# Gated linear attention with a maxout layer: constants made on chip, wider rows for the output matrix, fewer memsets and a new order of the work

## The chip, the cores and the metric

The kernel runs on one core of one Trainium2 chip. The core has five engines that follow their own instruction queues: TensorE (PE in the profile, its weight loads PEld), VectorE (DVE), ScalarE (ACT), GpSimd (POOL) and SyncE (SP), which here issues every DMA. The metric is the device time of one execution in microseconds, lower is better. The kernel before took 142.0 us, the median of three runs (141.97, 142.00 and 146.79).

## The reference

Inputs are `q`, `k`, `v` and `alpha` of shape (4, 8, 768, 48): batch, heads, tokens, head width; all float32. Then come three matrices of 384 x 768 and one of 768 x 384.

```
state = zeros(B, H, D, D)
for t in range(S):
    state = alpha[:, :, t, :, None] * state + einsum('bhd,bhe->bhde', k[:, :, t], v[:, :, t])
    y[:, :, t] = einsum('bhd,bhde->bhe', q[:, :, t], state)
x = y.transpose(0, 2, 1, 3).reshape(3072, 384)
h = maximum(maximum(x @ w1, x @ w2), x @ w3)
out = h @ w_out
```

The recurrence is a gated linear attention: a 48 x 48 state per batch and head, decayed row by row with `alpha` at each token. The second part is a maxout layer over 3072 tokens.

## The kernel before

**Staging.** The tokens are cut into 12 steps: step `s` is batch `s % 4` and 256 tokens of it. Within a step the 128 partitions hold pairs of neighbouring tokens (R = 2), and a step has two chunks (U = 2) of 128 tokens, each 64 partitions. The kernel takes logarithms of alpha, sums them within a chunk by one matmul with a signed triangle (`upto`), and turns the sums into scales for k and q by Exp (`decay_in`, `decay_out`). Scaled q and k are transposed (`turn` on PE for steps 0 to 4, `turn_by_dma` for the rest), multiplied to scores, masked with a causal mask while they leave PSUM (`masked`), and multiplied with v (`attend`). Between chunks runs the state: `update`, `add_state`, `decay_state`, `spread_state`.

**The maxout layer.** `max(x w1, x w2, x w3)` is written as `x w1 + max(0, x (w2 - w1), x (w3 - w1))`. So the kernel forms two differences `wdif` (pieces d0 to d5, two for each group of 256 hidden columns), multiplies x with them (`gate`, pieces G0 to G5 per step, twelve matmuls each), takes the maximum with zero and with each other (`maxed`), and projects (`project`): the hidden part with `wo16`, and x itself with `w1o`, the product of w1 and w_out, formed once on chip (`turn_weight`, `multiply_weights`). A step's gates thus need the differences, and each difference two blocks of weights of 384 KB (pieces K0 to K8, K9 to K11 for w_out). The weight blocks are staged in the ring slots 2 and 3 that later hold inputs, so a load of step 2 or 3 into such a slot waits until the differences have read it.

**Order.** Nothing is scheduled automatically. The string `ORDER` lists some 900 pieces: a letter for the function, an index, an engine (`v` DVE, `p` POOL, `a` ACT), `@` the step, and `#` the PSUM banks. Each engine, SP included, executes its pieces in this order; semaphores are put in by the framework. `l0` to `l3` load alpha, k, q and v of a step; rings have four slots per input, so a load waits for the last reader of the step four before. `H` are warm-up matmuls on a tile of zeros without effect on the output.

**Constants.** `ca` (the triangle `upto`, the selector `pick` and three columns of scales) and `cb` (identity and causal mask `pmask`) are computed on the host as part of the program and loaded by the pieces J0 and J1, the second and fourth issues on SP. `rowmask`, the mask in the row order of step 0, is copied from `pmask` by ACT.

**Padding.** Heads take 48 of 64 columns; the rest is cleared once by `clear_padding`: sixteen memsets for the state tiles and two for `la` on DVE, eleven for `vu`, `qk` and `vt` on POOL. They stand ahead of everything else in these engines' queues.

Of the kernel before, what the change touches and what calls it, by code (L numbers as in the profile page):

```python
# [9 lines left out]
FP32 = mybir.dt.float32  # L10
FP16 = mybir.dt.float16

# [11 lines left out]
def kernel(  # L24
# [39 lines left out]
    rr = np.arange(P)  # L64
    tri_np = (
        ((rr[:, None] > MID) & (rr[:, None] <= rr[None, :])).astype(np.float16)
        - ((rr[:, None] <= MID) & (rr[:, None] > rr[None, :])).astype(np.float16)
    )
    w2_np = np.stack([rr <= MID, rr > MID], 1).astype(np.float16)
    ur, jr = rr // J, rr % J  # L70
    same = (ur[:, None] == ur[None, :]).astype(np.float16)
    upto_np = same * np.tile(tri_np[R - 1::R, R - 1::R], (U, U))
    pick_np = np.zeros((P, U, 2), np.float16)
    for u in range(U):
        pick_np[u * J:(u + 1) * J, u] = w2_np[::R]
    token = np.concatenate([R * np.arange(J) + r for r in range(R)])
    pmask_np = (token[:, None] <= token[None, :]).astype(np.float16)
    at_pair = LAM * (R * jr + R - 1 - MID)
    at_token = LAM * (rr // R * R + R - 1 - MID)
    c32_np = np.stack(  # L80
        [np.exp(at_pair + SIGMA), np.exp(-at_token - SIGMA), 0 * rr - LAM * P / 2], 1
    ).astype(np.float32)
    ca_np = np.concatenate([np.concatenate([upto_np, pick_np.reshape(P, -1)], 1).view(np.float32), c32_np], 1)
    cb_np = np.concatenate([np.eye(P, dtype=np.float16), pmask_np], 1)

# [40 lines left out]
    rowmask = cpool.tile([P, R, P], FP16, name="rowmask")  # L126

    def load_const(_, i, eng):
        c, c_np = ((ca, ca_np), (cb, cb_np))[i]
        queues[eng].dma_start(c, nc.inline_tensor(c_np, name=f"c{i}").ap())  # L130

    half = ca.bitcast(FP16)
    upto, pick = half[:, :P], half[:, P:P + 2 * U]
    c32 = ca[:, P // 2 + U:]
    ident, pmask = cb[:, :P], cb[:, P:2 * P]
    vs_c, ys_c, undo_c = c32[:, 0:1], c32[:, 1:2], c32[:, 2:3]
# [6 lines left out]
    sts = [[cpool.tile([P, HP, 2, D], FP16, name=f"st{b}_{i}") for i in range(2)] for b in range(B)]  # L143

    def clear_padding():
        for st in (st for pair in sts for st in pair):
            for i in range(2):
                nc.vector.memset(st[64 * i:64 * (i + 1), :, 1 - i], 0.0)
        for la in las:
            nc.vector.memset(la.rearrange("p r a b c -> p (r a b) c")[:, :, D:], 0.0)  # L150
        for vu in vus:
            nc.gpsimd.memset(vu.rearrange("p u a b c -> p (u a b) c")[:, :, D:], 0.0)
        for qk, vt in zip(qks, vts):
            nc.gpsimd.memset(qk.rearrange("p r i a b c -> p (r i a b) c")[:, :, D:], 0.0)
            nc.gpsimd.memset(vt.rearrange("p a b c -> p (a b) c")[:, :, D:], 0.0)


# [69 lines left out]
    def sums(s, *_):  # L227
# [4 lines left out]
        for p in range(HP):  # L232
            for n, (r, _) in enumerate(parts):
                nc.tensor.matmul(lps(s, 1)[:, H * D + 2 * U * p:H * D + 2 * U * (p + 1)],
                                 las[s % 2][:, r, p].rearrange("p a b -> p (a b)"), pick,
# [71 lines left out]
    def spread_mask(_, i, eng):  # L307
        for u in range(U):
            for r in range(R):
                copy(eng, rowmask[u * J:(u + 1) * J, r], pmask[r * J:(r + 1) * J])  # L310

    def masked(s, x, eng):
# [5 lines left out]
        else:  # L318
            nc.vector.tensor_mul(lats[s % 2][u][:, i], bank(("aps", s, u, i), [HP, P]),  # L319
                                 pmask.unsqueeze(1).broadcast_to([P, HP, P]))  # L320
# [95 lines left out]
    def differ(_, i, eng):  # L416
        jg, g = divmod(i, 2)
        engines[eng].tensor_sub(  # L418
            wdif[:, :, g, column_group(jg)], staged(3 * jg + 1 + g).rearrange("p (f j) -> p f j", f=NF),
            staged(3 * jg).rearrange("p (f j) -> p f j", f=NF))  # L420

    def halve(_, i, eng):
        copy(eng, w1h[i], staged(3 * i).rearrange("p (f j) -> p f j", f=NF))
# [98 lines left out]
    def warm_after(n, name):  # L522
# [5 lines left out]
        "l": load_step, "J": lambda _, i, eng: load_const(0, 1 - i, eng), "I": spread_mask, "K": load_weight, "H": warm,  # L528
# [9 lines left out]
    def emit(order):  # L538
# [24 lines left out]
        x1a@2 c0@3#7 M1v@0 C2v@0 n2a@0 G4@2#6 G1@2#3 u0v@4 C0a@0 m0p@5 h5v@0 G3@2#0 l2@3 s1v@2 G2@2#2 C1v@0
        f0a@3 h4a@1 z1v@0 P0@0#1 h2v@2 h3v@2 P1@0#5 l3@4 k0p@4 N0a@5 h5v@1 r0a@3 P2@0#2 h4v@2 p0a@0 l3@3 r1a@3
        p1a@0 c0@5#0 p2v@0 G0@2#4 e0a@5 O1@0#6 h0a@2 g0a@5 w0v@4 q0v@4 e0a@3 T1@4#1 g0a@3 u0v@3 O0@1#5 o1a@0
        k0v@3 l0@7 y1a@0 l1@5 w0v@3 f0a@5 l0@8 r0a@5 q0v@3 T0@4#2 o0a@1 G5@2#4 t1a@4 M1v@1 V0v@4 l0@6 T0@3#7
        V0v@3 O0@0#6 t0a@3 h1v@2 v0p@3 l3@5 t0v@4 h5v@2 S0@4#0,5 v0p@4 o0a@0 S0@3#1,7 s0v@4 A0@4#3,2 s0v@3 l3@6
        T1@3#4 M0v@3 a1v@4 z0p@4 O0@2#6 l1@6 t1a@3 a0v@4 s1v@4 z0p@3 y0a@3 s1v@3 W1@0 m0p@7 A1@4#0,1 y0a@4
        A1@3#2,4 a2v@3 A0@3#3,5 a1v@3 O1@2#7 a3v@4 r0a@7 m0p@6 N0a@7 a3v@3 V0a@5 l2@5 u0p@5 c0@7#2 l2@6 O1@1#5
        N0a@6 r1a@5 a2v@4 v1p@3 l0@9 a0v@3 v1a@4 Y0@4#1 o1v@1 k0p@5 m0p@8 Y3@3#4 Y0@3#0 Y2@3 o0v@2 x0a@3 Y1@4  # L570
        W0@0 Y3@4#3 Y2@4 x1a@3 r0a@6 f0a@7 x0v@4 x1v@4 c0@6#5 G4@3#6 N0a@8 W0@2 w0v@5 G4@4#0 z1v@1 e0a@7 q0v@5
        f0a@6 r1a@6 w0p@6 D0@5 e0a@6 g0a@7 G0@4#4 h0a@4 G2@3#1 h2v@3 G3@3#3 V0a@6 r0a@8 G1@4#2 m0p@9 h4v@3 l2@7
        D1@5 c0@8#4 h3v@3 G5@3#1 q0p@6 g0a@8 N0a@9 h1v@4 G1@3#6 e0a@8 l1@7 o1v@2 c0@9#3 G0@3#2 h5v@3 M1p@4 g0a@6
        u0v@6 k0p@6 G2@4#7 r1a@7 h0v@3 f0a@9 G5@4#1 g0a@9 h1v@3 G3@4#5 v1a@5 h4a@4 h5v@4 O1@3#2 r0a@9 M1p@5 D0@6
# [61 lines left out]
```

## Time and profile before

| | |
|---|---|
| median of 3 runs | 142.0 us |
| the profiled execution | 143.14 us |
| its span | 141.4 us |
| PE / DVE / ACT / POOL busy | 130.9 / 116.7 / 96.0 / 65.4 us |
| warm-up matmuls, included in PE | 12.2 us |
| DMA traffic | 32.42 MB, mean 229 GB/s |

The profile comes from one execution, whose own time stands beside its span; the difference lies ahead of the first and behind the last recorded instruction. "L452" is line 452 of the kernel. `out<-in` names the tiles by the program's names, without buffer numbers, so `ra` is any of the four ring slots for alpha. A timeline row gives the start, the duration, the engine, the line, the operation, the tiles and shapes, and in brackets the idle time before it with what ended it; "x6" are six instructions merged.

### The profile page before, as it was taken

What the parts mean: (1) busy time and instruction counts of PE and PEld (TensorE: products, weight loads), DVE (VectorE), ACT (ScalarE), POOL (GpSimd) and SP (SyncE); (2) the same over time, 40 slices, a digit from 0 to 9 for tenths busy, and PEclk for the clock granted to TensorE, in tenths of its full rate; (3) what the DMA queues carried; (4) which work ended last, traced back from release to release, by engine and by line L of the source; (5) the groups of instructions that cost most, each with busy time, mean ns of one, the idle gap of its engine ahead of it and who ended that gap; (6) DMA issues with size and microseconds to landing.
All of it is one profiled execution on the core that took longest, in us unless ns stands there. A gap on an engine that the chain in (4) does not pass through costs nothing.

```text
span 141.4 us, 5309 instructions
## 1 busy us (share of the span) xinstructions
PE 130.9 (93%) x2238; PEld 94.6 (67%) x2238; DVE 116.7 (83%) x220; ACT 96.0 (68%) x202; POOL 65.4 (46%) x102
## 2 busy tenths in 40 slices
PE   6977697999998999999998999999999999999990
PEld 2434265787865676688767867787567876788670
DVE  5559979998999998979797987979989899847511
ACT  3667689999974978999997734497657480554121
POOL 8230171268080059939892999458507501700000
PEclk9999999999999999999999999999999999999998
DMA  4999999999996299998999899999999859401433
GB/s 111 273 333 349 298 261 335 321 326 365 302 282 173 52 322 320 278 308 151 230 216 228 250 188 291 272 169 233 197 267 318 182 112 257 154 5 63 159 111 111
DMA packets 73031, 32.42 MB, mean 229 GB/s; under 512 B 65456, under 2 KB 73008, under 8 KB 73008
## 3 DMA queue, kind: packets, MB, share of 16 engines
q1 hardware_dynamic: 73008, 32.09, 88.3%
q8 instruction: 17, 0.28, 0.7%
q14 instruction: 6, 0.05, 0.1%
HBM read 23.69 MB, written 4.72 MB: 201 GB/s over the span
## 4 chain that ended last, share of the span: by engine, by line
PE 51%; DMA 16%; DVE 16%; SPq 6%; POOL 3%; ACT 3%; issue 2%; DVEq 0%
PE bank L452 22%; PE bank L486 17%; DMA ra<-in_alpha_dram 5%; PE bank L330 5%; DMA rv<-in_v_dram 4%; DMA qkT<-qk 4%; DMA rq<-in_q_dram 3%; SPq L102 3%; PE bank L304 3%; DVE lat L319 2%; PE bank L283 2%; DVE qk L260 2%; DVE hT L461 2%; SPq L290 2%; PE bank L388 2%
## 5 line engine op out<-in xcount | busy, mean ns | idle before, releaser
L452 PE MATMUL bank<-xT,wdif 128*128 128x256 f16 x432 | 51.5, 273 | 0.3 <-DVE wdif L418 0.3
L452 PEld LDWEIGHTS <-wdif 128*128 128x128 f16 x432 | 40.7, 98 | 6.5 <-DVE wdif L418 0.6
L319 DVE TENSOR_TENSOR lat<-bank,cb 128x512 f16<-128x512 f32 x44 | 27.8, 682 | 1.5 <-PE bank L304 1.5
L486 PE MATMUL bank<-wo,hT 128*128 128x384 f16 (+1 forms) x150 | 27.5, 320 | 0.0
L461 DVE TENSOR_TENSOR hT<-bank,h 128x512 f16<-128x512 f32 x36 | 23.8, 686 | 3.9 <-PE bank L452 2.1
L486 PEld LDWEIGHTS <-hT 128*128 128x128 f16 x150 | 14.5, 98 | 9.0
L465 ACT ACTIVATE h<-bank 128x512 f16<-128x512 f32 x20 | 11.7, 601 | 7.9 <-PE bank L452 7.9
L486 PE MATMUL bank<-w1o,xT 128*128 128x384 f16 (+1 forms) x75 | 15.9, 320 | 0.0
L168 ACT ACTIVATE ob<-bank,ca 128x384 f32<-128x384 f32 (+1 forms) x15 | 8.4, 572 | 10.8 <-PE bank L486 8.0
L205 POOL TENSOR_TENSOR ra<-ra 128x384 f32<-128x384 f32 x9 | 9.0, 999 | 11.1 <-DMA ra<-in_alpha_dram 10.8
L505 PE MATMUL bank<-hT 128*128 128x512 f16 x41 | 12.2, 420 | 1.2 <-DVE hT L603 1.2
L463 DVE TENSOR_SCALAR h<-bank 128x512 f16<-128x512 f32 x16 | 10.7, 685 | 3.1 <-PE bank L452 3.0
L162 ACT CAST st<-kept 64x192 f16<-64x192 f32 x28 | 9.7, 347 | 4.9 <-POOL kept L404 4.7
L164 POOL COPY vu<-vt 64x384 f16<-64x384 f16 x16 | 8.0, 502 | 9.6 <-DVE vt L170 8.9
L162 ACT COPY vu<-vt 64x384 f16<-64x384 f16 x24 | 12.2, 509 | 0.4
L260 POOL TENSOR_TENSOR qk<-rq,ac 128x768 f16<-128x768 f32 x5 | 9.1, 1816 | 7.2 <-DVE rq L222 7.1
L260 POOL TENSOR_TENSOR qk<-rk,ic 128x768 f16<-128x768 f32 x5 | 9.4, 1877 | 2.3 <-DVE rk L219 1.6
L162 ACT CAST xT<-bank 128x384 f16<-128x384 f32 x14 | 6.3, 479 | 5.7 <-PE bank L330 5.7
L222 POOL TENSOR_TENSOR rq<-rq,ic 128x384 f32<-128x384 f32 x6 | 6.0, 1002 | 7.7 <-ACT ic L216 7.7
L304 PE MATMUL bank<-qkT 48*64 48x128 f16 x384 | 8.6, 219 | 0.7 <-DMA qkT<-qk 0.4
L170 DVE TENSOR_SCALAR ob<-bank,ca 128x384 f32<-128x384 f32 (+1 forms) x10 | 5.8, 591 | 3.8 <-PE bank L486 3.8
L168 ACT ACTIVATE vt<-rv,ca 128x768 f16<-128x768 f32 x8 | 7.5, 935 | 2.0 <-DMA rv<-in_v_dram 1.9
(82 smaller groups left out, 214.3 us busy)
## 6 DMA issues: line engine op xcount, KB each, us to landing
ra<-in_alpha_dram SPq DMA_DIRECT2D x12, 384.0 KB, 5.3
rk<-in_k_dram SPq DMA_DIRECT2D x12, 384.0 KB, 5.2
rv<-in_v_dram SPq DMA_DIRECT2D x12, 384.0 KB, 5.6
rq<-in_q_dram SPq DMA_DIRECT2D x12, 384.0 KB, 4.8
out_dram<-ob SPq DMA_DIRECT2D x23, 192.0 KB, 2.2
wst<-in_moe_w_out_dram SPq DMA_DIRECT2D x3, 384.0 KB, 6.1
ra<-in_moe_w_dram SPq DMA_DIRECT2D x2, 384.0 KB, 5.2
rk<-in_moe_w_dram SPq DMA_DIRECT2D x2, 384.0 KB, 6.2
```

The source lines that it names most:

```text
L162: nc.scalar.copy(out=dst, in_=src)
L168: nc.scalar.mul(dst, src, col)
L205: engines[eng].tensor_mul(raw("a", s, 0), raw("a", s, 0), raw("a", s, 1))
L260: engines[eng].tensor_mul(dst, src, by)
L304: nc.tensor.matmul(aps[i][to * J:(to + 1) * J, a * U + n, :], qkT[rows, r, 1, p, cols], qkT[rows, :, 0, p, cols], start=True, stop=True)
L319: nc.vector.tensor_mul(lats[s % 2][u][:, i], bank(("aps", s, u, i), [HP, P]), pmask.unsqueeze(1).broadcast_to([P, HP, P]))
L452: nc.tensor.matmul(gps[:, j, :], wdif[:, f, g, jj * P:(jj + 1) * P], xT[:, f].rearrange("p u t -> p (u t)"), start=(f == 0), stop=(f == NF ...
L461: nc.vector.tensor_max(hTs[s % NH][:, 2 * jg:2 * jg + 2, :], gps, h)
L463: nc.vector.tensor_scalar_max(h, gps, 0.0)
L465: nc.scalar.activation(out=h, in_=gps, func=AFT.Relu)
L486: nc.tensor.matmul(ops, lhs, (w1o if what == "x" else wo16)[:, j, cols], start=((what, j) == every[0]), stop=((what, j) == every[-1]))
L505: nc.tensor.matmul(wps, blank[:, :P], blank, start=True, stop=True)
```

## The change

Five things change together.

- **Constants.** `ca` and `cb` and their loads go. POOL makes an iota, a tile of ones and four selections (`affine_select`: keep ones where an affine function of partition and column meets a condition); DVE subtracts 1 in two blocks to make the signed triangle, fills `pick` and computes the exponents of the scales from the iota; ACT takes one Exp of two columns. `ident` and `pmask` are separate tiles.
- **w_out** is loaded with two neighbouring rows per partition, so 3 KB at a stretch in place of two rows of 1.5 KB. That permutes the hidden columns within a group of 256, and `differ` and `halve` write their results in the same permutation, pairs 128 columns apart.
- **Memsets.** The eight state tiles become slices of one tile `spread`, cleared by two memsets on DVE in place of sixteen. Five paddings go from POOL to ACT copies of zeros, two (`Z`) stand later in the order, four stay on POOL.
- **Order.** `ORDER` is another one from the first piece to the last. The set of pieces is the same but for J0 and J1, the two `Z` and the warm-ups (41 then, 39 now); some pieces change engine. The loads begin alpha 0, alpha 1, q 0, k 0, k 1, v 0 in place of alpha 0, `ca`, k 0, `cb`, v 0, alpha 1, q 0; then come three weight blocks.
- **Set-up order.** `clear_states`, `make_sums`, `make_masks`, `clear_padding` and `make_scales` stand ahead of `ORDER`, in this order.

```diff
-    ca = cpool.tile([P, P // 2 + U + 3], FP32, name="ca")
-    cb = cpool.tile([P, 2 * P], FP16, name="cb")
-    def load_const(_, i, eng):
-        c, c_np = ((ca, ca_np), (cb, cb_np))[i]
-        queues[eng].dma_start(c, nc.inline_tensor(c_np, name=f"c{i}").ap())
-                                  moe_w_out.rearrange("(j p) m -> p j m", p=P)[:, 2 * (i - 9):2 * (i - 8)])
+                                  moe_w_out.rearrange("(g p j) m -> g p j m", p=P, j=2)[i - 9])
+    def make_sums():
+        nc.gpsimd.iota(place_of, [[0, 1]], base=0, channel_multiplier=1)
+        nc.gpsimd.memset(ones, 1.0)
+        nc.gpsimd.affine_select(upto, ones, [[1, P]], AOP.is_ge, 0.0, base=0, channel_multiplier=-1)
+        nc.vector.memset(upto[:J, J:], 0.0)
+        for u in range(U):
+            block = upto[u * J:u * J + J // 2, u * J:(u + 1) * J]
+            nc.vector.tensor_scalar_add(block, block, -1.0)
+    def make_scales():
+        nc.vector.memset(pick, 0.0)
+        for u in range(U):
+            for i in range(2):
+                nc.vector.memset(pick[u * J + i * J // 2:u * J + (i + 1) * J // 2, u, i:i + 1], 1.0)
+        nc.vector.memset(undo_c, -LAM * P / 2)
+        at = LAM * (R - 1 - MID)
+        nc.vector.tensor_single_scalar(place_in[:, 0:1], place_of, J - 1, AOP.bitwise_and)
+        nc.vector.tensor_single_scalar(place_in[:, 1:2], place_of, P - R, AOP.bitwise_and)
+        nc.vector.tensor_scalar(vs_c, place_in[:, 0:1], R * LAM, at + SIGMA, AOP.mult, AOP.add)
+        nc.vector.tensor_scalar(ys_c, place_in[:, 1:2], -LAM, -at - SIGMA, AOP.mult, AOP.add)
+        nc.scalar.activation(out=c32[:, 0:2], in_=c32[:, 0:2], func=AFT.Exp)
+    def make_masks():
+        nc.gpsimd.affine_select(ident, ones, [[1, P]], AOP.is_equal, 0.0, base=0, channel_multiplier=-1)
+        for r in range(R):
+            rows = slice(r * J, (r + 1) * J)
+            nc.gpsimd.affine_select(pmask[rows], ones[rows].rearrange("p (r j) -> p r j", r=R),
+                                    [[r, R], [1, J]], AOP.is_ge, 0.0, base=-r, channel_multiplier=-1)
-        for st in (st for pair in sts for st in pair):
-            for i in range(2):
-                nc.vector.memset(st[64 * i:64 * (i + 1), :, 1 - i], 0.0)
         for la in las:
             nc.vector.memset(la.rearrange("p r a b c -> p (r a b) c")[:, :, D:], 0.0)
+        zeros = blank.rearrange("p (a c) -> p a c", c=64 - D)
         for vu in vus:
-            nc.gpsimd.memset(vu.rearrange("p u a b c -> p (u a b) c")[:, :, D:], 0.0)
-        for qk, vt in zip(qks, vts):
+            nc.scalar.copy(out=vu.rearrange("p u a b c -> p (u a b) c")[:, :, D:], in_=zeros[:, :U * H])
+        for vt in vts[2:]:
+            nc.scalar.copy(out=vt.rearrange("p a b c -> p (a b) c")[:, :, D:], in_=zeros[:, :R * H])
+        for qk, vt in zip(qks[:2], vts):
             nc.gpsimd.memset(qk.rearrange("p r i a b c -> p (r i a b) c")[:, :, D:], 0.0)
             nc.gpsimd.memset(vt.rearrange("p a b c -> p (a b) c")[:, :, D:], 0.0)
+    def clear_states():
+        for i in range(2):
+            nc.vector.memset(spread[64 * i:64 * (i + 1)].rearrange("p x b a i d -> p (x b a) i d")[:, :, 1 - i], 0.0)
     def differ(_, i, eng):
-            wdif[:, :, g, column_group(jg)], staged(3 * jg + 1 + g).rearrange("p (f j) -> p f j", f=NF),
-            staged(3 * jg).rearrange("p (f j) -> p f j", f=NF))
+            wdif[:, :, g, column_group(jg)].rearrange("p f (j n) -> p f n j", j=2), staged(3 * jg + 1 + g).rearrange("p (f n j) -> p f n j", f=NF, j=2),
+            staged(3 * jg).rearrange("p (f n j) -> p f n j", f=NF, j=2))
     ORDER = """
-        l0@0 J1@0 l1@0 J0@0 l3@0 l0@1 r0a@0 m0v@0 l2@0 N0a@0 r1a@0 u0v@0 H15@0#0 c0@0#0 g0a@0 e0a@0 K0@0 f0a@0
-        k0v@0 l1@1 V0v@0 K2@0 H6@0#1 H1^k0@0#1 S0@0#1,2 K1@0 l2@1 I0a@0 r0a@1 m0p@1 l3@1 M0p@0 N0a@1 w0v@0 q0v@0
+        l0@0 m0v@0 l0@1 l2@0 l1@0 r0a@0 l1@1 N0a@0 H10@0#0 c0@0#0 l3@0 g0a@0 r1a@0 M0p@0 f0a@0 K1@0 m0p@1 N0a@1
+        H7@0#1 c0@1#1 I0a@0 K0@0 w0p@0 q0v@0 K2@0 e0a@0 l2@1 u0v@0 l3@1 k0v@0 H3@0#2 H4^q0@0#2 T0@0#2 r0a@1
+        e0a@1 f0a@1 g0a@1 l0@4 V0a@0 u0v@1 M0v@1 k0v@1 H1@0#3 S0@0#3,4 t0v@0 s0a@0 r1a@1 z0v@0 T1@0#5 t1a@0
...
     with tc.manual_schedule():
         nc.vector.memset(blank, 0.0)
+        clear_states()
+        make_sums()
+        make_masks()
         clear_padding()
+        make_scales()
         emit(ORDER)
```

The pieces in the order that the prediction speaks of: `m` pair product of alpha, `r`, `N` logarithms, `c` the decay sum on PE, `e`, `f` the scales for k and q, `g` totals, `M` gates between chunks, `w`, `u` the first products of q and k, `q`, `k` their scaling, `V`, `v` the values, `T`, `t` transposes and their copies, `A`, `a` scores and masks, `Y`, `x` outputs and their copies.

More of the change, by code (lines that the diff above doesn't have):

```diff
@@ L11 @@
 FP16 = mybir.dt.float16
+I32 = mybir.dt.int32
 AOP = mybir.AluOpType
@@ L62 @@
     assert S % W == 0 and U * J == P and (MID + 1) % R == 0
[L64 to L84, printed above, removed]
     cpool = ctx.enter_context(tc.tile_pool(name="const", bufs=1))
@@ L132 @@
[L132 to L135, printed above, removed]
-    vs_c, ys_c, undo_c = c32[:, 0:1], c32[:, 1:2], c32[:, 2:3]
+                                  moe_w_out.rearrange("(g p j) m -> g p j m", p=P, j=2)[i - 9])
+    upto = cpool.tile([P, P], FP16, name="upto")
+    pick = cpool.tile([P, U, 2], FP16, name="pick")
+    ident = cpool.tile([P, P], FP16, name="ident")
+    pmask = cpool.tile([P, R, J], FP16, name="pmask")
@@ new lines @@
+    rowmask = cpool.tile([P, R, P], FP16, name="rowmask")
+    ones = cpool.tile([P, P], FP16, name="ones")
+    place_of = cpool.tile([P, 1], I32, name="place_of")
+    place_in = cpool.tile([P, 2], I32, name="place_in")
+    c32 = cpool.tile([P, 3], FP32, name="c32")
+    vs_c, ys_c, undo_c = c32[:, 0:1], c32[:, 1:2], c32[:, 2:3]
+    def make_sums():
[6 more added lines that the diff above has]
+            nc.vector.tensor_scalar_add(block, block, -1.0)
@@ L309, in spread_mask @@
             for r in range(R):
-                copy(eng, rowmask[u * J:(u + 1) * J, r], pmask[r * J:(r + 1) * J])
+                copy(eng, rowmask[u * J:(u + 1) * J, r], pmask[r * J:(r + 1) * J].rearrange("p r j -> p (r j)"))
     def masked(s, x, eng):
@@ L527 @@
     pieces = {
[L528 removed]
+        "l": load_step, "I": spread_mask, "Z": clear_pairs, "K": load_weight, "H": warm,
         "m": pair_decay, "N": logs, "r": inverse, "u": near_k, "w": near_q,
```

111 lines of the change are left out of this document (59 added, 52 removed).

## The prediction

> **What bounds the kernel now.** I read the page's first two parts first, then the busy time by stretch, then the timelines of the first 48 us.
>
> ```profile
> span 141.4 us, 5309 instructions
> PE 130.9 (93%) x2238; PEld 94.6 (67%) x2238; DVE 116.7 (83%) x220; ACT 96.0 (68%) x202; POOL 65.4 (46%) x102
> ...
> DMA  4999999999996299998999899999999859401433
> ```
>
> The view by stretch has, per row: length, then PE, PEld, DVE, ACT and POOL busy, the clock, the DMA share and GB/s. The last row is the same view for line 505 alone, the warm-up matmuls.
>
> ```profile
> 0.00:26.00 26.00, 20.39 (x321) 10.98 (x322) 19.62 (x48) 18.41 (x38) 8.70 (x22) 1.00 0.98 278
> 26.00:47.00 21.00, 20.11 (x309) 15.31 (x308) 20.23 (x34) 17.57 (x37) 9.48 (x9) 1.00 0.96 283
> 47.00:71.00 24.00, 24.00 (x452) 18.23 (x455) 21.91 (x41) 22.02 (x48) 16.82 (x24) 1.00 0.99 247
> 71.00:120.00 49.00, 48.45 (x910) 36.15 (x895) 44.23 (x83) 30.36 (x66) 27.53 (x42) 1.00 1.03 227
> 120.00:141.40 21.40, 17.93 (x272) 13.97 (x270) 10.70 (x18) 7.63 (x16) 2.87 (x6) 0.98 0.29 103
> ...
> 0.00:26.00 26.00, 12.22 (x41) 3.77 (x41) 1.00 0.98 278
> ```
>
> From 26 us on PE is busy for 20.11 + 24.00 + 48.45 + 17.93 = 110.5 of 115.4 us, and most of the missing 4.9 us is the drain after the last matmul. Before 26 us only 20.39 - 12.22 = 8.2 us are real work; the rest is warm-up or waiting. So the time is: when PE gets fed, plus 110 us of packed PE, plus a tail. An edit that changes no matmul can gain only in the head or in the 0.9 us that PE idles between 26 and 47 us, where DVE is busy for 20.23 of 21 us and so nearly as tight. The DMA engines are full too until 120 us, apart from a gap before 50 us that is taken up below.
>
> **The change, part by part.** *Constants.* Two loads go from SP's queue, and loads of steps 0 and 1 change places. The first two rows are the issues on SP, the others show when a load landed, by who had been waiting for it.
>
> ```profile
> 1.26 0.56 SPq L130 DMA_DIRECT2D ca<-c  x1
> 2.33 0.92 SPq L130 DMA_DIRECT2D cb<-c  x1
> ...
> 10.07 0.56 DVE L222 TENSOR_TENSOR rq<-rq,ic 128x384 f32<-128x384 f32 x1 [1.64 <-DMA rq<-in_q_dram]
> 16.53 0.56 DVE L222 TENSOR_TENSOR rq<-rq,ic 128x384 f32<-128x384 f32 x1 [0.32 <-DMA rq<-in_q_dram]
> ...
> 19.42 1.00 POOL L205 TENSOR_TENSOR ra<-ra 128x384 f32<-128x384 f32 x1 [0.44 <-DMA ra<-in_alpha_dram]
> ```
>
> The 5th large load (q of step 0) lands at 10.0, the 10th (q of step 1) at 16.5, the 12th (alpha of step 4) at 19.4: (19.4 - 10.0)/7 = 1.34 us each. The first lands at 4.3 (below). The 5th would by this pace land at 4.3 + 4 x 1.34 = 9.7, so the two constants cost 0.3 us of transfer; their 1.5 us on SP were covered by queued loads. I gain 0.3 us on every landing of the head: alpha 0 at 4.3, alpha 1 5.6, q0 7.0, k0 8.3, k1 9.7, v0 11.0, three weight blocks to 15.0, q1 16.4. The weights K4, K3, K5, which the third gate group needs, stay loads 14 to 16: the last lands near 4.3 + 15 x 1.34 = 24.4, against 24.7 by the same pace before.
>
> *Masks, memsets and scales.* What now stands ahead of the first decay sum:
>
> ```profile
> 0.86 0.27 DVE L603 MEMSET hT<- 128x256 uint32 x1 [0.86 <-PEq L620]
> 1.09 3.08 DVE L148 MEMSET st<- 64x96 uint32 x16
> 4.25 0.31 DVE L150 MEMSET la<- 128x128 uint32 x2
> 4.47 0.49 DVE L205 TENSOR_TENSOR ra<-ra 128x384 f32<-128x384 f32 x1
> ...
> 0.73 1.28 ACT L89 ACT_TABLE_LOAD   x1 [0.73 <-PEq L620]
> 4.34 0.52 ACT L214 ACTIVATE ic<-ra 128x384 f32<-128x384 f32 x1 [2.33 <-DMA ra<-in_alpha_dram]
> 5.00 0.52 ACT L209 ACTIVATE la<-ra 128x384 f16<-128x384 f32 x1
> 7.17 1.21 ACT L162 COPY rowmask<-cb 64x128 f16<-64x128 f16 x4
> ...
> 5.81 0.33 PE L231 MATMUL bank<-la,ca 128*128 128x384 f16 x1
> ```
>
> On DVE the sixteen memsets cost 3.08 us. The two new ones write 768 words per partition each: by the hT row (256 words, 0.27) at most 0.81, by the slope between 128 words (half of 0.31) and 256 words, 0.9 ns a word, 0.74; I take 0.75 each. DVE then stands at 1.1 + 1.5 = 2.6 us and waits for the triangle from POOL. After it come three small operations on the triangle, the two `la` memsets (0.31), and ten operations of one to four columns. No row has these; the 128x4 product of gates is the nearest (0.15 below, 0.07 where the next one follows at once), the old memset at 3.08/16 = 0.19 the upper end. Thirteen at 0.07 to 0.19 are 0.9 to 2.5; I take 0.12, 1.6 us. DVE is free at 2.6 + 0.3 + 1.6 = 4.5 against 4.47 before. ACT gets five copies of padding: by the `rowmask` row 0.30 for half as many columns, so about 0.4 each (0.3 to 0.5), 2.0 us from the end of the table load at 2.0, thus 4.0: under the wait for alpha. Then an Exp of two columns (0.27 at most by the 128x16 totals) which waits for DVE: 4.8. `la` can start at 5.1 and the first decay sum, which came 0.81 us after it, at 5.9 against 5.81. So this part costs nothing if POOL's triangle is there by 2.6 us.
>
> POOL:
>
> ```profile
> 0.34 0.10 POOL L620 MEMSET const-uint8-127<- 128x1 uint8 x1
> 4.10 0.31 POOL L155 MEMSET vt<- 128x256 f16 x1
> 8.90 1.00 POOL L205 TENSOR_TENSOR ra<-ra 128x384 f32<-128x384 f32 x1 [4.49 <-DMA ra<-in_alpha_dram]
> ...
> L205 POOLq MODIFY_POOL_CONFIG  x2: 11/11/11, 4.4 to 4.4; - x2
> ...
> 8.85 0.52 ACT L214 ACTIVATE ic<-ra 128x384 f32<-128x384 f32 x1 [0.48 <-DMA ra<-in_alpha_dram]
> 37.25 0.15 DVE L377 TENSOR_TENSOR gm<-ge,ge 128x4 f32<-128x4 f32 x1
> ```
>
> From 0.7 us: an iota (0.10 to 0.2), a memset of 128 columns (0.2, between 0.10 and 0.31), one selection of 128 columns. No selection is in the trace: between that memset (0.2) and a third of the 384-column product (1.00/3 = 0.33), at worst a whole such product; I take 0.33. The triangle is there at about 1.5 us, 1.1 us before DVE asks. But before its first operation that is not a memset POOL now executes the configuration that stood at 4.4 us. What follows it can cost from nothing to 8.90 - 4.4 = 4.5 us: the next operation started 4.5 us later, but 0.05 us after ACT, which waited for the same alpha. It could have been over long before. I take nothing, and price the upper end as a rival.
>
> The Trainium skill speaks against this edit: GPSIMD Engine Reference, section 2.1, says that the first call to a freshly loaded kernel pays some 6 us of code load that no instruction shows. The trace allows 4.5 us at most for this one, so the figure does not hold here; whether a part of it does no run shows yet.
>
> *Up to the gates.* From 5.9 us, with 0.4 us a plain ACT operation, 1.0 a POOL product, 0.9 a scaled q or k on DVE (the 0.96 rows of line 260): r1 6.9, f0 7.3, POOL's m0@1 7.8 and w0@0 8.8, q of step 0 9.8; the row-mask copies hold ACT until 9.5, e0 9.9, k 11.1, transposes 11.6, v0 (landed 11.0) scaled by 12.1, scores near 14.5, against 15.5 before. DVE then does d0, d1 and step 1's q (landed 16.4, done 17.9), three masks, two copies: step 0's x stands at 21.5, against 23.4.
>
> ```profile
> 23.48 0.82 PE L452 MATMUL bank<-xT,wdif 128*128 128x256 f16 x6
> 24.86 0.96 DVE L418 TENSOR_TENSOR wdif<-rq,rv 128x768 f16<-128x768 f32 x1
> 25.88 0.83 PE L452 MATMUL bank<-xT,wdif 128*128 128x256 f16 x6 [0.31 <-DVE wdif L418]
> ...
> 42.98 1.14 PE L440 MATMUL bank<-wo,w1T 128*128 128x384 f16 x6 [0.70 <-DVE h L463]
> ...
> 31.25 1.81 POOL L418 TENSOR_TENSOR wdif<-wst,rk 128x768 f16<-128x768 f32 x1
> 33.90 2.14 PE L452 MATMUL bank<-xT,wdif 128*128 128x256 f16 x18
> ```
>
> The first gate matmul so comes 2 us earlier, but the work that packs PE begins with the third group, at 25.88, behind d3. There d3 started at 24.86, right behind other DVE work. Afterwards DVE has finished its masks by 22.6, d2 waits for K3 (23.0) and d3 for K5 (24.4): d3 done 25.3, group three at 25.3. Ahead of it stands the same PE work except for one sum. **Gain 0.6 us.** More is not to be had while the weights land when they do.
>
> *Weights between 26 and 47 us.* The differences are now written in pairs 128 columns apart. On DVE the reading of two float32 operands sets 0.96, and line 260 writes pieces of 48 at the same 0.96: I take no change (at the upper end as much again on four, 3.8 us of DVE, part of it on the path; so far only a stall rival). On POOL d4 and d5 take 1.81 each, and the new writing costs between nothing and half as much again (0.9 each); d5 ended 0.84 us before the groups of line 452 at 33.90 began, which hides one of the two; beyond that PE would wait. I take none. Halving moves from DVE (0.55) to ACT (0.82), as do one copy of w_out and six of the 16 maxima with zero over the whole kernel (0.69 each on DVE); DVE gets some copies back. PE's 0.70 us wait for DVE at 42.98 should mostly go: **gain 0.5**, bounds 0 and the 0.9 of this stretch. The 3 KB rows change three loads of 384 KB among 60: at most a few tenths of a load, under full PE.
>
> *From 47 us.* The order differs everywhere, the work does not; PE has 0.55 us of idle to win up to 120 us, and as much can be lost at any hand-over. I take zero. One move helps: SP's idle gap goes.
>
> ```profile
> 38.82 2.53 SPq L102 DMA_DIRECT2D rv<-in_v_dram  x2
> 47.45 0.37 SPq L102 DMA_DIRECT2D ra<-in_alpha_dram  x1
> ```
>
> From 41.35 to 47.45 SP stood at alpha of step 7, whose ring slot is freed by u0@3 on DVE. In the new order alpha 6 and 8 and k5, whose slots are free, go first: about 3 loads, 4 us of transfer, are ahead of need. PE was full there, so this is worth nothing by itself; it covers a PE that runs a microsecond earlier. The tail (last projection, scale, store) has the same pieces, its scaling on DVE in place of ACT: zero.
>
> **Sum:** 0.6 + 0.5 = 1.1 us off the profiled execution's 143.14 (span 141.4 and 1.74 around it), 142.0; against the median of 142.0 that is **140.9**. I use the median, as the profiled execution was 0.8% above it.
>
> **Rivals.** *The landings and DVE decide as before* (no change): if the small DVE operations take 0.19 each, DVE is free 0.9 us later, the lead at the third group is spent, and moved work costs DVE what it saved: 142.0. For it: DVE at 20.23 of 21. *The configuration on POOL is paid for* (slower): with all 4.5 us the triangle is there at 5.9, not 1.5. It decides from 1.1 us upwards, since DVE has no use for it before 2.6. In DVE's order the product of alpha (m0@0) stands behind it, and the Exp that needs it ahead of ACT's first logarithm: first sum at 9.3. Following the chain as above, k ends at 14.6, step 1's q at 21.2, x at 24.9, and alpha 2's load, which needs d0 and d1 done, is issued at 19.8 in place of 16.3; d3 ends at 27.9. Group three is 2.1 us later than 25.88: 144.1, and up to 145 if PE, without work from 4.4 to 9.3, then gets a lower clock. By TensorE: Matmul & The Clock Gate in the Trainium skill (section 1, the clock gate), an idle window of about 3.4 us halves the clock; PE's longest wait by the row below is 1.2 us, so no row here shows it. Against it: no transfer and no late start is seen at 8.90. *New stalls*: hand-overs that are late by 0.3 us in each of nine steps are 2.7 us, 144.7; for it, all of DVE, PE and the queues are near full; against it, before loses 0.55 us in 49. *More than I count*: between 18 and 26 us PE had 8.00 - (6.71 - 1.35) = 2.6 us without real work; if two thirds of that go, and all 0.9 later, it is 2.6 us and 139.4.
>
> ```profile
> PE bank L505 <- DVE hT L603: 1.2, 1, 1.2
> ...
> 18.00:26.00 8.00, 6.71 (x185) 4.46 (x184) 7.12 (x14) 7.33 (x16) 2.83 (x5) 1.00 1.01 294
> ...
> 18.00:26.00 8.00, 1.35 (x5) 0.21 (x3) 1.00 1.01 294
> ```
>
> The first row is PE's longest wait, the others the stretch from 18 to 26 us, whole and for line 505 alone.
>
> **Chances.** Forecast 0.48 (its own range 140.0 to 141.8); no change 0.19; configuration 0.13; stalls 0.11; more 0.09. Range 139.3 to 144.5: below it lies the larger part of the last case, should more than two thirds go, above it a part of configuration and of stalls. A measurement of this kernel tells about 2% from no change: 139.2 and 144.8. Faster by more: 0.08. Slower: 0.05 from configuration with a lower clock, 0.07 from stalls, 0.12. Within: 0.80.
>
> **What would show it.** The POOL timeline: selections of about 0.33 us from 1 us, and no hole behind the configuration. First sum near 5.9, first gate near 21.5, third group near 25.3, its releaser DVE behind a weight load. PE busy 20.5 or more between 26 and 47 us. SP without a gap at 41 to 47 us. A first sum after 7.5, or PE idle of more than 2 us between 47 and 130, would make the forecast wrong.

## The result: 161.3 us, 14% slower

The changed kernel took 161.31 us (median of 6 runs, 160.9 to 163.24) against 141.99 us for the kernel before, a ratio of 1.142 with a 95% interval of 1.133 to 1.151. The ratio compares the means of the fast runs alone, which leaves out two of the six runs of the kernel before (143.19 and 146.79). The forecast was 140.9 with a range of 139.3 to 144.5. It was wrong, and nearly all of that by one term.

The page of the changed kernel, its first two parts (the slices are fortieths of the span), then the busy time by stretch with the columns explained in the prediction:

```profile
span 159.4 us, 5314 instructions
PE 137.2 (86%) x2233; PEld 99.0 (62%) x2233; DVE 129.6 (81%) x223; ACT 108.5 (68%) x216; POOL 66.6 (42%) x91
...
PE   6878269626965999999999969999999999999991
...
PEclk9999655985899599999999999999999999999999
```

```profile
0.00:26.00 26.00, 18.09 (x190) 9.15 (x191) 20.39 (x37) 17.70 (x33) 7.39 (x20) 0.84 0.74 213
26.00:47.00 21.00, 13.57 (x229) 9.93 (x226) 19.13 (x17) 14.39 (x24) 14.99 (x9) 0.80 0.85 265
47.00:71.00 24.00, 22.06 (x349) 16.53 (x347) 19.10 (x38) 22.48 (x42) 4.58 (x9) 0.93 0.67 179
```

From slice 14 (52 us) on PE is full but for 1.5 us in slice 24 and the drain at the end, so nearly everything is lost ahead of 52 us. Between 26 and 47 us PE is busy for 13.57 us where it was 20.11, and does it at a granted clock of 0.80, while DVE is still at 19.13 of 21: with 17 instructions, where it had 34. So single instructions of DVE have become long. Selected rows of the timelines of DVE, ACT, POOL, PE and SP name them:

```profile
14.50 3.55 DVE L434 TENSOR_TENSOR wdif<-rq,ra 128x768 f16<-128x768 f32 x1
18.49 3.60 DVE L434 TENSOR_TENSOR wdif<-rk,ra 128x768 f16<-128x768 f32 x1
33.10 4.18 DVE L434 TENSOR_TENSOR wdif<-rq,rv 128x768 f16<-128x768 f32 x1
40.49 3.46 DVE L235 TENSOR_TENSOR rk<-rk,ra 128x384 f32<-128x384 f32 x1
...
15.59 3.65 ACT L178 CAST ob<-ra 128x768 f16<-128x768 f32 x1
35.05 5.22 POOL L434 TENSOR_TENSOR wdif<-rv,rk 128x768 f16<-128x768 f32 x1 [1.19 <-DMA rk<-in_moe_w_dram]
39.86 4.18 POOL L434 TENSOR_TENSOR wdif<-wst,rk 128x768 f16<-128x768 f32 x1
...
19.29 0.82 PE L445 MATMUL bank<-ident,ob 128*128 128x128 f16 x6 [2.97 <-ACT ob L178]
33.55 0.83 PE L468 MATMUL bank<-xT,wdif 128*128 128x256 f16 x6 [2.73 <-DVE wdif L434]
37.33 1.46 PE L468 MATMUL bank<-xT,wdif 128*128 128x256 f16 x6 [2.95 <-DVE wdif L434]
...
11.44 11.09 SPq L81 DMA_DIRECT2D ra<-in_alpha_dram  x2
```

A difference of weights takes 3.55 us on DVE where it took 0.96, a halving 3.65 on ACT where it took 0.82, and POOL's differences 5.22 and 4.18 where they took 1.85 and 1.81. These are exactly the operations that now write pairs 128 columns apart. The number of elements and their types are the same. The product at 40.49 has no such writing; it took 3.46 us in place of 0.55 while POOL's second difference ran beside it. The second gate group starts at 33.55 and the third at 37.33, where the forecast had 25.3 for the third (a gate piece is six matmuls, as in these rows, not twelve). The long differences hold back the loads as well: alpha 2 goes where the first two differences read, the second of them ends at 22.1, and SP stands at the two issues of alpha until 22.5 us; the DMA share of the first stretch is 0.74 where it was 0.98. How much of the loss goes this way was not taken apart.

### The profile page after: what moved, and what is told of

Read it like the earlier page. It is cut to its first block, busy times and chain, and to the rows that moved or that the text cites. A ratio compares the mean times of both kernels' runs of the same rounds, so it can differ in the third digit from the quotient of the medians.

```text
span 159.4 us, 5314 instructions
## 1 busy us (share of the span) xinstructions
PE 137.2 (86%) x2233; PEld 99.0 (62%) x2233; DVE 129.6 (81%) x223; ACT 108.5 (68%) x216; POOL 66.6 (42%) x91
## 4 chain that ended last, share of the span: by engine, by line
PE 57%; DVE 18%; issue 8%; ACT 5%; POOL 4%; DMA 3%; SPq 2%; DVEq 0%; POOLq 0%; ACTq 0%
PE bank L468 22%; PE bank L502 20%; DVE wdif L434 5%; PE bank L346 5%; DVE qk L276 5%; DVE rk L235 3%; PE bank L299 3%; PE bank L320 3%; DMA out_dram<-ob 3%; ACT ob L178 2%; SPq L306 2%; PE bank L404 2%; PE bank L456 2%; DVE lat L335 2%; DVE ob L186 1%
## 5 line engine op out<-in xcount | busy, mean ns | idle before, releaser
L335 DVE TENSOR_TENSOR lat<-bank,pmask 128x512 f16<-128x512 f32 x44 | 28.2, 686 | 2.6 <-PE bank L320 1.8
L481 ACT ACTIVATE h<-bank 128x512 f16<-128x512 f32 x26 | 15.3, 604 | 8.8 <-PE bank L468 8.4
L276 POOL TENSOR_TENSOR qk<-rk,ic 128x768 f16<-128x768 f32 x6 | 10.9, 1822 | 6.1 <-DVE rk L235 5.0
L184 ACT ACTIVATE ob<-bank,c 128x384 f32<-128x384 f32 (+1 forms) x13 | 7.2, 566 | 9.0 <-PE bank L502 5.4
L276 DVE TENSOR_TENSOR qk<-rq,ac 128x768 f16<-128x768 f32 x8 | 8.9, 1109 | 3.9 <-POOL rq L238 3.7
L178 ACT CAST spread<-kept 64x192 f16<-64x192 f32 x28 | 9.8, 349 | 3.0 <-POOL kept L420 2.6
L186 DVE TENSOR_SCALAR ob<-bank,c 128x384 f32<-128x384 f32 (+1 forms) x12 | 7.1, 597 | 5.5 <-PE bank L502 3.6
L184 ACT ACTIVATE vt<-rv,c 128x768 f16<-128x768 f32 x9 | 8.6, 956 | 3.4 <-DMA rv<-in_v_dram 3.4
L180 DVE CAST xT<-bank 128x384 f16<-128x384 f32 x11 | 6.0, 554 | 5.2 <-PE bank L346 5.2
L299 PE MATMUL bank<-ident,qk 128*128 128x128 f16 x80 | 6.8, 237 | 3.3 <-DVE qk L276 3.3
L276 POOL TENSOR_TENSOR qk<-rq,ac 128x768 f16<-128x768 f32 x4 | 7.3, 1816 | 5.5 <-ACT la L225 5.4
```

Of the source, the lines that this page charges most:

```text
L178: nc.scalar.copy(out=dst, in_=src)
L180: engines[eng].tensor_copy(out=dst, in_=src)
L184: nc.scalar.mul(dst, src, col)
L276: engines[eng].tensor_mul(dst, src, by)
L299: nc.tensor.transpose(tps[:, i, p, :], qks[s % NQ][:, r, i, p].rearrange("p a b -> p (a b)"), ident)
L481: nc.scalar.activation(out=h, in_=gps, func=AFT.Relu)
```

## The experiments

The theory after this reading was that the write pattern is the whole loss. The rival was that the new order or the constants on chip lose as well, perhaps most of it.

**The permutation undone, the rest of the change kept.** The halving is changed back in the same way.

```diff
-                                  moe_w_out.rearrange("(g p j) m -> g p j m", p=P, j=2)[i - 9])
+                                  moe_w_out.rearrange("(j p) m -> p j m", p=P)[:, 2 * (i - 9):2 * (i - 8)])
-            wdif[:, :, g, column_group(jg)].rearrange("p f (j n) -> p f n j", j=2), ...
+            wdif[:, :, g, column_group(jg)], staged(3 * jg + 1 + g).rearrange("p (f j) -> p f j", f=NF),
...
```

> The changed kernel with the permutation of the hidden columns undone: w_out in rows of 1.5 KB, differences and halves written in order; constants, memsets and the new order stay. Theory W (the writing in pairs 256 bytes apart is what the change costs): one difference takes 0.96 us on DVE again in place of 3.55, the third gate group starts near 25.3, and the time is 140.9 as predicted for the rest, 139.5 to 142.5. Rival O (the new order and the constants on chip lose by themselves): at least 148, with PE idle that has another releaser than the differences.

Measured: 1.013 times before (1.006 to 1.019). Of 14.2% loss 12.9 points are gone with these lines. What is left is a loss of about 1.3%, not the gain of 0.8% that was forecast for the rest, and above the 139.5 to 142.5 expected for this run.

**The permutation alone, in the old order.** The same lines, put into the kernel before.

> The kernel before with only the permutation: w_out in rows of 3 KB, differences and halves written in pairs. Theory W: four differences on DVE at 3.55 in place of 0.96 and two on POOL at 4.2 to 5.2 in place of 1.85 are 15 to 17 us on the path between 14 and 45 us; one halving on DVE instead of ACT; 155 to 162. Rival O: the permutation costs little in an order that was not made for it, under 148.

Measured: 1.146 (1.137 to 1.154). The permutation by itself is as slow as the whole change; the median of 163.58 us is a little above the 155 to 162 expected. The order theory is out as the main cause. One row of the groups by shape and one of PE's waits:

```profile
L418 DVE TENSOR_TENSOR wdif<-ra,rv 128x768 f16<-128x768 f32 x1 | 3.5, 3548 | 0.0
...
PE bank L452 <- DVE wdif L418: 5.4, 2, 3.0
```

**The same permutation, run in the order of the result.** Both kernels compute the same; only which side of the operation jumps differs.

```diff
-            wdif[...].rearrange("p f (j n) -> p f n j", j=2), staged(...).rearrange("p (f n j) -> p f n j", f=NF, j=2),
+            wdif[...].rearrange("p f (j n) -> p f j n", j=2), staged(...).rearrange("p (f n j) -> p f j n", f=NF, j=2),
...
```

> The changed kernel with the same permutation, but the differences and halves run in the order of the result: they write one column after the other and read every second float, 8 bytes apart. Theory W says that the writing is dear and the reading is not: 0.96 us for a difference, 140 to 142. If any access that is not in order costs (rival S), a difference takes 2 us or more and the time is over 148.

Measured: 1.011 (1.005 to 1.018), median 143.71, above the 140 to 142 expected but far from 148, with a difference on DVE at 0.95 us again. Reading every second float is free for DVE's differences; writing in pairs is not. This kernel is also the cleanest test of the prediction's other steps, and these lines of its timelines and of its view by stretch carry them:

```profile
6.21 0.48 PE L247 MATMUL bank<-la,upto 128*128 128x384 f16 x1 [0.51 <-ACT la L225]
22.21 0.81 PE L468 MATMUL bank<-xT,wdif 128*128 128x256 f16 x6
25.91 0.83 PE L468 MATMUL bank<-xT,wdif 128*128 128x256 f16 x6 [0.51 <-DVE wdif L434]
...
24.89 0.96 DVE L434 TENSOR_TENSOR wdif<-rq,rv 128x768 f16<-128x768 f32 x1 [0.37 <-DMA rq<-in_moe_w_dram]
10.98 6.51 SPq L81 DMA_DIRECT2D ra<-in_alpha_dram  x2
...
26.00:47.00 21.00, 21.00 (x335) 16.99 (x336) 19.29 (x36) 20.59 (x46) 8.42 (x8) 1.00 1.00 290
71.00:120.00 49.00, 46.75 (x858) 35.12 (x857) 43.58 (x86) 30.32 (x66) 26.77 (x37) 1.00 1.04 230
...
74.59 0.42 PE L320 MATMUL bank<-qkT 48*64 48x128 f16 x16 [0.60 <-DMA qkT<-qk]
75.55 0.43 PE L404 MATMUL bank<-vt,qk 64*64 64x48 f16 x30 [0.52 <-ACT ob L184]
76.32 0.82 PE L468 MATMUL bank<-xT,wdif 128*128 128x256 f16 x6 [0.35 <-ACT xT L178]
```

First sum at 6.2 (forecast 5.9), first gate at 22.2 (21.5), PE full between 26 and 47 us (20.5 or more). But the third group is at 25.9, no earlier than before, and between 71 and 120 us PE idles for 2.25 us where it idled 0.55.

**The permutation moved to PE's weight loads.** The transposes of w1 read in the same way.

```diff
-                nc.tensor.matmul(gps[:, j, :], wdif[:, f, g, jj * P:(jj + 1) * P],
+                nc.tensor.matmul(gps[:, j, :], wdif[:, f, g, column_group(jg)].rearrange("p (n j) -> p j n", j=2)[:, j],
...
```

> The changed kernel with w_out in rows of 3 KB, differences and halves written in order, and the permutation moved to PE: the weight loads of the gates and of the transposes of w1 read every second column, 4 bytes apart. Theory W: DVE as in the run with the permutation undone. If a weight load does not care about the step, 140 to 142; if it takes twice as long (100 ns to 200 ns for 432 loads), PE loses up to 40 us.

Measured: 1.026 (1.017 to 1.034), not the 140 to 142 us expected for a weight load that does not care. Yet a weight load with every second column takes what it took, 99 ns against 98:

```profile
L468 PEld LDWEIGHTS <-wdif 128*128 128x128 f16 x432 | 41.6, 99 | 11.3 <-POOL wdif L434 2.6 <-DVE wdif L434 2.1 <-issue 0.6
L434 POOL TENSOR_TENSOR wdif<-rv,rk 128x768 f16<-128x768 f32 x1 | 1.8, 1810 | 5.0 <-PE bank L468 5.0
```

The loss against the run with reading pairs goes with a wait: POOL's first difference stood 5.0 us for a gate matmul of PE, and PE later 2.2 in two waits for POOL's differences, as much as it idled between 26 and 47 us. Which rule of the framework puts this wait there was not tried.

**The constants alone, in the old order.** The order of before without its two constant loads; constants, scales and memsets as changed; hidden columns in order.

> The order of before without the two loads of constants, with the constants, scales, masks and memsets of the changed kernel, the hidden columns in order. If the constants made on chip are neutral, as the prediction's sum had it (first decay sum at 5.9 against 5.81), 141.5 to 142.5; if they cost what is left of the loss (about 1 us), the first sum comes later than 6.2 and the third gate group too, 143 to 144.

Measured: 0.999 (0.994 to 1.003), although the first sum came at 6.96 us in its trace, 1.15 later than before. Constants on chip and the two memsets are worth nothing and cost nothing that this interval would show.

**The new order with the constants loaded.**

```diff
-        l0@0 m0v@0 l0@1 l2@0 l1@0 r0a@0 l1@1 N0a@0 H10@0#0 ...
+        l0@0 J1@0 m0v@0 l0@1 J0@0 l2@0 l1@0 r0a@0 l1@1 N0a@0 H10@0#0 ...
```

> The changed kernel with the hidden columns in order and the constants loaded again, as the second and fourth large-step issues of the queue; the new order and the two memsets stay. If the new order is what loses the last 1%, 143.5 to 145 as with the constants on chip; if the constants on chip lose it, 141.5 to 142.5.

Measured: 1.014 (1.005 to 1.024). With the constants either way the new order loses some 1.2%.

**Wide rows alone, old order, reading every second float.**

> The kernel before with w_out in rows of 3 KB and the differences and halves reading every second float, writing in order. The wide rows change three loads of some sixty, under a full PE: 142.0, 141.4 to 142.6.

Measured: 1.007 (1.002 to 1.012), a small loss; the median of 143.06 us is above the 141.4 to 142.6 expected. Reading every second float makes other operations longer than DVE's differences. Groups by shape, mean ns behind the comma:

```profile
L418 POOL TENSOR_TENSOR wdif<-rv,rk 128x768 f16<-128x768 f32 x1 | 2.3, 2298 | 2.2 <-DMA rv<-in_moe_w_dram 2.2
L164 DVE CAST ob<-ra 128x768 f16<-128x768 f32 x1 | 0.9, 946 | 0.0
```

POOL's difference took 1.85 in order, DVE's halving 0.55. Whether these or the wide rows cost the 0.7% is not shown: in this run's trace PE waits for POOL once, for 0.87 us at 10.7 us, long before POOL's differences.

**What a write costs.** Single operations behind the kernel's end, on otherwise idle engines, on scratch.

```diff
+        nc.scalar.copy(out=pairs(s16, 4), in_=plain(x, 4))     # half words alternating 8 bytes apart; 16 is the next line
+        nc.scalar.copy(out=wide[:, :, 0], in_=x)               # every second half word
+        nc.scalar.copy(out=pairs(s32, 128), in_=plain(x, 128)) # float32 alternating 512 bytes apart
...
```

> The changed kernel with the hidden columns in order, and behind its last piece a row of single operations of 768 columns on DVE, ACT and POOL that write scratch: in order, alternating between two places 4, 8, 16, 32, 64, 128, 256 and 768 bytes apart, every second half word, float32 in order and alternating 512 bytes apart, and reading alternately. Theory W1 (a lone half word that does not continue the last write costs, whatever the distance): 0.96 in order, 3.5 for every alternation and for the step of two. W2 (it costs only where the next write falls outside a word or line of some size): 0.96 up to some distance, 3.5 beyond it. Whether float32 is free of it is open: 0.96 if the half word is the reason, 3.5 if the jump is.

Groups by shape of that run; the lines are, on ACT, in order, then alternating 8 and 16 bytes apart, every second half word, float32 in order, float32 alternating, and reading alternately; then POOL alternating 8 and 16 bytes apart:

```profile
L651 ACT CAST rk<-wst 128x768 f16<-128x768 f32 x1 | 0.8, 832 | 0.0
L653 ACT CAST rk<-wst 128x768 f16<-128x768 f32 x1 | 0.8, 831 | 0.0
L654 ACT CAST rk<-wst 128x768 f16<-128x768 f32 x1 | 3.6, 3590 | 0.0
...
L660 ACT CAST rk<-wst 128x768 f16<-128x768 f32 x1 | 1.3, 1337 | 0.0
L661 ACT COPY rk<-wst 128x768 f32<-128x768 f32 x1 | 0.8, 819 | 0.0
L662 ACT COPY rk<-wst 128x768 f32<-128x768 f32 x1 | 1.5, 1517 | 0.0
L663 ACT CAST rk<-wst 128x768 f16<-128x768 f32 x1 | 1.0, 977 | 0.0
...
L669 POOL TENSOR_TENSOR rq<-wst,wst 128x768 f16<-128x768 f32 x1 | 1.8, 1800 | 0.1
L670 POOL TENSOR_TENSOR rq<-wst,wst 128x768 f16<-128x768 f32 x1 | 3.6, 3597 | 0.1
```

There is a threshold, as W2 had it: up to 8 bytes apart the alternation is free, at 16 bytes it costs 3590/768 = 4.7 ns a half word, and nearly the same on ACT, POOL and DVE at every larger distance tried (3547 to 3612 ns an operation). The row of every second half word (1337) is not such a cost: it starts 0.5 us before the scattered write ahead of it has ended. Float32 has the cost less, 1517/768 = 2.0 ns on ACT, and on POOL not at all, 1817 ns against 1799 in order.

**Runs and steps, on DVE.**

```diff
+        nc.vector.tensor_sub(s16.rearrange("p (j n c) -> p n j c", j=2, c=2), ...)      # alternating in runs of c
+        nc.vector.tensor_sub(w16.rearrange("p (n k) -> p n k", k=8)[:, :, 0], ...)      # one stream, step of k half words
...
```

> The changed kernel with the hidden columns in order, and behind it single operations on DVE that write scratch: 768 half words alternating between two places in runs of 1, 2, 4, 8, 16, 32; then one stream of half words with a step of 4, 8, 16, 32 and 64 bytes, and of float32 with a step of 4 to 64 bytes. If a write pays per 16 bytes that it begins, not per element, runs of 2, 4 and 8 take about a half, a quarter and an eighth of 3.55 (not under 0.96), and a single stream with a step of 16 bytes or more costs 4.6 ns an element like the alternation. If only going to and fro costs, the single streams stay near 1.2 ns an element at every step.

Groups by shape: alternating 768 bytes apart in runs of 1 and of 2; one stream of half words with steps of 4, 8, 16 and 32 bytes; float32 with steps of 16 and 32 bytes:

```profile
L630 DVE TENSOR_TENSOR ra<-wst,wst 128x768 f16<-128x768 f32 x1 | 3.5, 3545 | 0.0
L631 DVE TENSOR_TENSOR ra<-wst,wst 128x768 f16<-128x768 f32 x1 | 1.0, 959 | 0.0
...
L636 DVE TENSOR_TENSOR ra<-wst,wst 128x768 f16<-128x768 f32 x1 | 1.0, 1004 | 0.0
L637 DVE TENSOR_TENSOR ra<-wst,wst 128x384 f16<-128x384 f32 x1 | 1.0, 1009 | 0.0
L638 DVE TENSOR_TENSOR ra<-wst,wst 128x192 f16<-128x192 f32 x1 | 1.0, 1006 | 0.0
L639 DVE TENSOR_TENSOR ra<-wst,wst 128x96 f16<-128x96 f32 x1 | 0.6, 558 | 0.0
...
L643 DVE TENSOR_TENSOR ra<-wst,wst 128x192 f32<-128x192 f32 x1 | 0.5, 499 | 0.0
L644 DVE TENSOR_TENSOR ra<-wst,wst 128x96 f32<-128x96 f32 x1 | 0.3, 331 | 0.0
```

768, 384 and 192 half words with steps of 4, 8 and 16 bytes all take 1.0 us: they begin the same 192 pieces of 16 bytes (the first of the three proves little, since 768 in order take 0.95). From 192 to 96 pieces the time falls by (1006 - 558)/96 = 4.7 ns a piece; for float32 by (499 - 331)/96 = 1.8 ns. So going to and fro is not the reason: on DVE a write pays per 16 bytes that it begins, 4.7 ns when half words lie alone in them and some 2 ns when whole words do. The expectation for runs of two, about 1.8 us, was too timid: two half words side by side are enough to bring the operation back to 0.96 us. By estimate from these rows, 384 pieces at 2 ns would be 0.8 us and so hidden under the 0.95 that the operation takes in order.

**Which engine's writing costs the time.** The kernel that reads every second float, with the writing in pairs put back for DVE's four differences only, for ACT's three halves only, and for POOL's two differences only.

```diff
+        if eng == "v":
+            engines[eng].tensor_sub(wdif[...].rearrange("p f (j n) -> p f n j", j=2), ...)
+        else:
             engines[eng].tensor_sub(wdif[...].rearrange("p f (j n) -> p f j n", j=2), ...)
```

> The kernel that reads every second float, with only the four differences on DVE written in pairs again. The loss of the change against that kernel is 17.6 us. Theory D (DVE alone is on the path): four differences at 2.6 us more are 10.4, the loss is 10 to 13. Theory P (the engines' costs add): the same here, and the rest in the two runs beside it.

> The same with only ACT's three halves written in pairs. They are 2.7 us longer each, 8.1 in all. Theory D: ACT has little room between 26 and 47 us, half of it shows, 3 to 5 us. Theory P: 5 to 8 us.

> The same with only POOL's two differences written in pairs. They are 1.4 to 3 us longer each, and DVE's operations with two operands in SBUF stood still beside them in the changed kernel (a product of 0.55 took 3.46). Theory D: POOL is off the path, at most 2 us. Theory P: 3 to 5 us, by that standstill and by the gates that wait.

Measured against before: 1.088 (1.078 to 1.099) for DVE, 1.077 (1.070 to 1.084) for ACT, 1.019 (1.011 to 1.026) for POOL. From each goes the 1.011 of the kernel without any: 7.7, 6.6 and 0.7 points, or about 10.9, 9.3 and 1.0 us. The last is no larger than the two intervals allow by chance. They sum to 15.0 points where all three together cost 13.1, so they add up about, and may overlap a little. DVE's cost and POOL's are as theory D had them. Both theories missed on ACT: eight microseconds of longer copies cost nine. PE's longest waits, of the first run and of the second:

```profile
PE bank L299 <- DVE qk L276: 5.9, 2, 5.6
PE bank L473 <- DVE wdif L435: 5.5, 2, 2.8
```

```profile
PE bank L404 <- ACT vt L184: 3.1, 3, 1.9
PE bank L445 <- ACT ob L178: 2.9, 1, 2.9
PE bank L247 <- ACT la L225: 2.8, 4, 1.1
```

With ACT alone slow, PE waits for values, halves and logarithms in turn: everything behind a long copy in ACT's queue. No kernel tried beats the kernel before; the constants alone tie with it.

## Why the prediction was wrong

**The step that failed** is "On DVE the reading of two float32 operands sets 0.96, and line 260 writes pieces of 48 at the same 0.96: I take no change (at the upper end as much again on four, 3.8 us of DVE, ...)", with POOL's "half as much again" and the halving's 0.82 on ACT. The term was 0 with an upper end of about 4 us of DVE; measured it is 2.6 us on three of DVE's differences and 3.2 on the fourth, 2.8 on each of three halves, and 3.4 and 2.4 on POOL's. Together they cost 13.1 points, some 18 us, against the kernel that differs in this alone (1.142 and 1.011). The row that was used as a neighbour, line 260, writes runs of 48 half words; the new pattern writes runs of one. Runs of two were free on DVE. The halving was priced by its old row, although its pattern changed in the same way; that price had no upper bound at all. So the range, too, was built on a neighbour that did not share the property that mattered.

**Masks and set-up: right.** The lines of the changed kernel on POOL:

```profile
L115 POOLq MODIFY_POOL_CONFIG  x2: 11/11/11, 0.8 to 0.8; - x2
...
0.90 0.13 POOL L115 IOTA place_of<- 128x1 int32 x1 [0.39 <-POOLq L640]
1.25 0.29 POOL L117 TENSOR_SCALAR_AFFINE_SELECT upto<-ones 128x128 f16<-128x128 f16 x1
```

A selection of 128 columns took 0.29 (0.33 was taken), the triangle was there at 1.5, the two memsets took 0.70 each (0.75). DVE was free at 5.0 in place of 4.5, as the two subtractions in the triangle took 0.79 us and had been priced at 0.12 each; the first sum came 0.3 us late. The rival of the pool configuration is dead: the iota started 0.1 us behind it. By GPSIMD Engine Reference, section 2.1, of the Trainium skill a first call after a load pays some 6 us; the trace shows no such cost here, and no run shows whether this configuration loads any code.

**The gain of 0.6 at the third group: not there.** The walk to the first gate was right to 0.7 us. But the last weight block of the group landed at 24.9, not 24.4 (its row in the third experiment: DVE waits 0.37 for it). The loads of alpha 4 and alpha 2 held SP until 17.5 us (10.98 + 6.51), since alpha 2 goes where the first block is staged and the second difference reads that until 17.0; the sum had it ended at 16.3. Only the landing pace was counted there, not the issue. With the constants loaded the third group is at 25.81: the 0.3 us of landing was not there either.

**The gain of 0.5 between 26 and 47 us: right** (PE 21.00 of 21, 0.9 in fact). This is the kernel with reading pairs. SP's gap closed as forecast there: its issues follow each other from 35 to 57 us.

**Zero from 47 us: wrong by 1.7 us.** In that kernel PE idles 2.25 us between 71 and 120, of which the three rows at 74.6 to 76.3 are 1.47; the stalls rival had the sign, its size was 2.7. The first of them is a transpose by DMA for step 5, the others behind ACT. With the constants loaded the same three waits are there (0.42, 0.50 and 0.35 us), and constants loaded or made, the order loses 1.1 to 1.4%. Why the transposes come late in it was not tried.

**Constants and memsets at zero: right** (0.999). **Wide rows under a full PE at zero: open.** With the reading that they ask for they cost 0.7% in the old order, and nothing in the new one (1.011 with both, 1.013 with neither); which of the two costs it was not tried.

**The clock.** PE's granted clock of 0.84 and 0.80 in the first two stretches adds to the loss: PE is busy for 137.2 us where it was 130.9, with two warm-ups fewer. Its waits before the halves and before the second and third gate group are near 3 us each. TensorE: Matmul & The Clock Gate, Part 1, in the Trainium skill puts the lower clock behind an idle window of about 3.4 us; the longest single wait here is 2.97, so the trace shows the lower clock behind shorter waits. It fell to 0.50 at 17.5, 34.6 and 51.6 us, and in the 3.4 us ahead of these moments PE had been busy for 1.9, 0.8 and 1.5 us. What share of the loss is the clock's was not taken apart.

## What to carry to other kernels

Look at the innermost run of what an operation writes: float16 results laid one by one into places 16 bytes or more apart cost 4.7 ns each here, on DVE, ACT and POOL, and on DVE a run of four bytes ended that. Turn the loops so that the jump is on the reading side, which cost far less here, and price a changed access pattern by a row with the same run length, not by one with the same element count. The wider rows of three loads, for which the pattern was changed, brought nothing that these runs could show.

## What the runs showed of the hardware

- The cost of lone half words is the same 4.7 ns on DVE, ACT and POOL (3.55 to 3.61 us for 768). On DVE it goes with 16-byte pieces: 192 pieces cost 1.0 us whether they get one or two half words each with gaps between.
- Float32 alternating 512 bytes apart costs near 2.0 ns an element on ACT and DVE, 1.9 and 1.5 times its time in order, and nothing more on POOL. Reading alternately is free on DVE, 0.98 against 0.83 on ACT, and 2.78 against 1.80 on POOL:

```profile
L679 POOL TENSOR_TENSOR rq<-wst,wst 128x768 f16<-128x768 f32 x1 | 2.8, 2782 | 0.0
```

- A product of two SBUF operands on DVE stood for 3.46 us (0.55 alone) beside a long difference on POOL, which with the writing in pairs lasts 4.2 us. A product on POOL took 3.09 us (1.00 alone) beside a long difference on DVE. Why was not tried.
